# A hand-written engine order for the first 32 units of an attention and FFN kernel, with the weights' low words converted in place

## The chip, the cores and the metric

The kernel runs on one core of one Trainium2 chip. The metric is the device time of one execution in microseconds (us). A core has a matrix engine (TensorE, PE in the profile), whose weight loads are listed apart as PEld, and three engines for element-wise work: VectorE (DVE), ScalarE (ACT) and GpSimd (POOL). SyncE (SP) issues the transfers between HBM and the core's memory. Each engine works through its own queue in order; an instruction waits for others by semaphores.

## The reference, cut to what matters

Local and global attention over 8 batches, 8 heads, 512 local and 32 global tokens, head size 64; its output, 4352 rows of 512, goes through a feed-forward network with a leaky activation, all in fp32.

```python
s_g = scale * q_g @ k_all.T            # global tokens see all 544 keys
out_g = softmax(s_g) @ v_all
s_ll = where(abs(i - j) <= 32, scale * q_l @ k_l.T, -1e9)
s_lg = scale * q_l @ k_g.T
out_l = softmax(concat([s_lg, s_ll])) @ concat([v_g, v_l])
x = concat([out_g, out_l])             # rows of 8 heads * 64
h = x @ w_in                           # 512 -> 2048
g = maximum(h, 0) + alpha * minimum(h, 0)
out = g @ w_out                        # 2048 -> 512
```

The weights are handed to the kernel as 64-bit floating-point numbers. Each is decoded on the chip from its high and its low 32-bit word into an fp32 number, which is then split into a rounded part and the rest, so that three TensorE products stand for one exact fp32 product.

## The kernel before, in words

The program is one loop over units u = 0 to 164, written out in full. An attention job is a pair of heads P (32 pairs: four for each batch), and every pair takes four units, s = 0 to 3 (P, s = divmod(u, 4)). From unit 19 on (NPRE) a unit also carries one step t = u - 19 of the feed-forward network: `f1(t)` multiplies 128 hidden channels for a batch of 512 rows (12 matmuls into the PSUM tile h_ps, two buffers), and `f2(t-2, part)` takes the activated result of two steps before into the four output banks (12 matmuls, tiles o). Sixteen steps make a batch, and batch b needs pairs 4b to 4b+3. The first 19 units hold attention alone, and in them `keep_warm` issues five matmuls on a zeroed tile per unit.

Pairs below 8 (NRAW) take the "raw" path, which this change is mostly about. At s=0 six score blocks of two heads are multiplied, masked and exponentiated (`scores_raw`, `softmax`: one DVE instruction and one ACT exponential each, lines 202 to 207); at s=1 the last two blocks follow, along with the transposed global probabilities of the pair before (`transpose_glb`, `copy_glb`, line 286); at s=2 the pair before is multiplied with its values (`pv_raw`), the global scores are multiplied (`global_scores`) and `pv_out` copies the result out (lines 359 to 367); then `global_softmax` runs a chain of five small DVE instructions, an exponential, four small DVE instructions and a scaling (lines 267 to 277). The `tail` of a softmax (lines 209 to 216) adds an epsilon on ACT, takes the reciprocal on DVE and normalizes the eight blocks on ACT; for pair 0 three of them run on GpSimd (line 214). At s=3 TensorE transposes the probabilities (`transpose_pe`), ACT copies them (line 302) and DVE transposes the small remainders (line 315). Pairs share one p_sb and one pt_sb buffer. Pairs from 8 on take another path, by way of HBM.

Weights come in 32 pieces of 128x512 numbers, two for each of the 16 hidden blocks. A piece is loaded six pieces ahead (`load_weights`, line 99), decoded by `decode_words` (two ACT instructions, lines 107 and 108, three on DVE, lines 109 to 112, a GpSimd addition, line 114), and one unit later split by `split_weights` (ACT, line 120, GpSimd, line 121). From unit 3 on the pace is one piece in two units out of three; from unit 19 on one or two in turn (RATE).

The order on TensorE is the written one: `matmul` and `transpose` pin every instruction behind the one before. On ACT, DVE, GpSimd and in the queue of DMA issues, a planner orders the instructions by its own estimate of their times, with higher priority for attention from unit 4 on (`boost`). Scratch tiles of 128x512 come from one ring of 18 buffers, tag "st" (`stage`): the two decode tiles wt and wr, the activation tiles g, gh and gl, the split inputs xh and xl, the tile vx of extra values of a raw pair, a mask and an identity. Larger tiles come from 33 buffers of the pool wpool: raw and split weights, and rawk.

Of the kernel before, what the change touches and what calls it, by code (L numbers as in the profile page):

```python
# [38 lines left out]
NPRE = 19  # L39
LAG = 2  # L40
WFIRST = 3
RATE = ((1, 1, 0), (2, 1))
# [9 lines left out]

@with_exitstack
def longformer_ffn(ctx: ExitStack, tc: tile.TileContext, qk, qkr, gn, vt, vx, w, alpha, out):
    nc = tc.nc
    PS = bass.MemoryType.PSUM
# [46 lines left out]
    def decode_words(f, j):  # L103
        words = wraw.pop((f, j)).rearrange("p (n two) -> p n two", two=2)
        low, high = words[:, :, 0], words[:, :, 1]
        t, r = stage("wt"), stage("wr", I32)
        nc.scalar.activation(t, high.bitcast(F32), AF.Abs)  # L107
        nc.scalar.activation(r, low, AF.Copy, scale=2.0**-29)
        nc.vector.tensor_scalar(t, t, CLAMP_LO, CLAMP_HI, op0=ALU.max, op1=ALU.min)  # L109
        tu = t.bitcast(U32)  # L110
        nc.vector.tensor_scalar(tu, tu, 3, 0x3FFFFFFF, op0=ALU.logical_shift_left, op1=ALU.bitwise_and)  # L111
        nc.vector.scalar_tensor_tensor(tu, high, 0xC0000000, tu, op0=ALU.bitwise_and, op1=ALU.bitwise_or)  # L112
        ti = t.bitcast(I32)
        nc.gpsimd.tensor_tensor(ti, ti, r, op=ALU.add)  # L114
        wmid[f, j] = t

    def split_weights(f, j):
        t = wmid.pop((f, j))
        wt = wpool.tile([128, 2, 512], F32R, tag="w", name="wt")
        nc.scalar.copy(wt[:, 0, :], t)  # L120
        nc.gpsimd.tensor_tensor(wt[:, 1, :], t, wt[:, 0, :].bitcast(F32), op=ALU.subtract)
# [9 lines left out]
    nc.vector.memset(rmask[0:64, 0, 0:32], NEG)  # L131
    nc.vector.memset(rmask[64:128, 2, 128:160], NEG)
# [5 lines left out]
    nc.vector.memset(idle.bitcast(F32), 0.0)  # L138
# [25 lines left out]
    def load_v(P):  # L164
# [4 lines left out]
        if P < NRAW:  # L169
            vxs[P] = stage("vx").rearrange("p (i n) -> p i n", i=4)  # L170
            nc.sync.dma_start(vxs[P], vx[P])
# [5 lines left out]
    def prep_qk(P, h, part):  # L177
# [6 lines left out]
        nc.scalar.copy(t, raw)  # L184
        if part == 0:
            q = t[64:128]
            nc.gpsimd.tensor_tensor(q, raw[64:128], q.bitcast(F32), op=ALU.subtract)  # L187
        else:
            kl[P, h] = work.tile([128, NK], F32R, tag="kl", name="kl", bufs=2)
            nc.gpsimd.tensor_tensor(kl[P, h], raw, t.bitcast(F32), op=ALU.subtract)  # L190
# [8 lines left out]
    def softmax(parts, npool=0):  # L199
        n = len(parts)  # L200
        mn, z, rz = small("mn", 6), small("z", 6), small("rz", 6)
        for e, (src, mk, pr) in enumerate(parts):
            nc.vector.tensor_tensor_reduce(  # L203
# [3 lines left out]
            nc.scalar.activation(pr, pr, AF.Exp, bias=mn[:, e : e + 1], scale=-1.0, accum_out=z[:, e : e + 1])  # L207

        def tail():
            nc.scalar.activation(rz[:, 0:n], z[:, 0:n], AF.Copy, bias=1e-9)  # L210
# [276 lines left out]
    def attn_mid(u):  # L487
# [4 lines left out]
        if P >= NRAW:  # L492
            while tails:
                tails.pop()()
# [158 lines left out]
```

## Time and profile before

| | us |
|---|---|
| median of 3 runs | 1026.85 (1025.22 to 1028.45) |
| the profiled execution | 1027.97 |
| its span, first to last instruction | 1026.20 |

The mean granted TensorE clock of the profiled execution is 0.972 of full speed. Busy over the span: PE 980.9 us, DVE 624.0, ACT 528.3, GpSimd 410.9. In the profile's rows a group reads as line, engine, operation, tiles written and read, shape and count, then busy time, mean ns of one, and the idle time ahead of them with what ended it. Rows of the view by windows give busy time of each engine in a stretch, with the granted clock (PEclk) and the share of the DMA engines in use.

### The profile page before, as it was taken

What the parts mean: (1) busy time and instruction counts of PE and PEld (TensorE: products, weight loads), DVE (VectorE), ACT (ScalarE), POOL (GpSimd) and SP (SyncE); (2) the same over time, 40 slices, a digit from 0 to 9 for tenths busy, and PEclk for the clock granted to TensorE, in tenths of its full rate; (3) what the DMA queues carried; (4) which work ended last, traced back from release to release, by engine and by line L of the source; (5) the groups of instructions that cost most, each with busy time, mean ns of one, the idle gap of its engine ahead of it and who ended that gap; (6) DMA issues with size and microseconds to landing.
All of it is one profiled execution on the core that took longest, in us unless ns stands there. A gap on an engine that the chain in (4) does not pass through costs nothing.

```text
span 1026.2 us, 16973 instructions
## 1 busy us (share of the span) xinstructions
PE 980.9 (96%) x5615; PEld 792.2 (77%) x5615; DVE 624.0 (61%) x1975; ACT 528.3 (51%) x1476; POOL 410.9 (40%) x332
## 2 busy tenths in 40 slices
PE   5589998879999999999999999999999999999998
PEld 3356776658888888888888888888888888888798
DVE  7735878776666766676666666666667665322322
ACT  5676767556555655555556555555556543201121
POOL 6601676764344443334434344334434422222222
PEclk8688999889999999999999999999999999999999
DMA  9624522234544544555445544554445532100010
GB/s 348 248 82 142 189 100 92 80 91 143 151 151 144 168 151 142 151 152 174 142 143 160 181 141 141 152 173 144 134 145 179 152 108 84 42 1 1 1 43 21
DMA packets 95274, 133.00 MB, mean 130 GB/s; under 512 B 10193, under 2 KB 53713, under 8 KB 95185
## 3 DMA queue, kind: packets, MB, share of 16 engines
q1 hardware_dynamic: 95184, 131.91, 41.1%
q8 instruction: 44, 0.72, 0.3%
q14 instruction: 46, 0.37, 0.1%
HBM read 100.93 MB, written 30.93 MB: 129 GB/s over the span
## 4 chain that ended last, share of the span: by engine, by line
PE 83%; DVE 7%; ACT 5%; issue 2%; DMA 1%; POOL 1%; SPq 0%; DVEq 0%; ACTq 0%; POOLq 0%
PE h_ps L84 35%; PE o L84 34%; PE o_ps L84 5%; PE s_ps L84 4%; PE g_ps L84 3%; ACT p_sb L207 2%; DVE wt L112 1%; DVE wt L109 1%; DVE wt L111 1%; PE warm L84 1%; ACT p_sb L216 1%; DMA wraw<-in_w_dram 1%; ACT wt L107 1%; DVE g L395 1%; DVE pt_sb L315 1%
## 5 line engine op out<-in xcount | busy, mean ns | idle before, releaser
L84 PE MATMUL h_ps<-xh,wt 128*128 128x512 f32 (+1 forms) x1152 | 350.4, 387 | 5.5 <-ACT wt L120 3.1
L399 POOL TENSOR_TENSOR gl<-g,gh 128x512 fp32r<-128x512 f32 (+1 forms) x144 | 177.6, 1233 | 426.6 <-ACT gh L398 378.1
L84 PE MATMUL o<-gh,wt 128*128 128x512 f32 (+1 forms) x1152 | 284.9, 390 | 0.0
L84 PEld LDWEIGHTS o<-gh,wt 128*128 128x128 f32 x1152 | 208.0, 190 | 45.6 <-issue 0.7
L84 PEld LDWEIGHTS h_ps<-xh,wt 128*128 128x128 f32 x1152 | 206.9, 190 | 44.5 <-ACT wt L120 3.3
L398 ACT CAST gh<-g 128x512 fp32r<-128x512 f32 (+1 forms) x144 | 85.3, 593 | 273.3 <-DVE g L396 266.2
L84 PE MATMUL h_ps<-xl,wt 128*128 128x512 f32 (+1 forms) x576 | 221.9, 385 | 0.9 <-DVE xl L378 0.9
L395 DVE TENSOR_SCALAR g<-h_ps,alpha_sb 128x512 f32<-128x512 f32 (+1 forms) x144 | 103.2, 717 | 147.1 <-PE h_ps L84 143.5
L84 PE MATMUL o<-gl,wt 128*128 128x512 f32 (+1 forms) x576 | 151.2, 385 | 0.0
L207 ACT ACTIVATE p_sb<-p_sb,mn 128x224 f32<-128x224 f32 (+2 forms) x256 | 115.0, 451 | 45.2 <-DVE mn L203 45.2
L216 ACT ACTIVATE p_sb<-p_sb,rz 128x192 f32<-128x192 f32 (+1 forms) x253 | 100.3, 451 | 71.7 <-DVE rz L211 66.8
L84 PEld LDWEIGHTS h_ps<-xl,wt 128*128 128x128 f32 x576 | 109.1, 189 | 24.4 <-DVE xl L378 1.1
L84 PEld LDWEIGHTS o<-gl,wt 128*128 128x128 f32 x576 | 106.4, 191 | 23.7
L297 DVE STREAM_TRANSPOSE pt_sb<-sg_sb 32x64 f32<-32x64 f32 x384 | 90.5, 236 | 26.8 <-ACT sg_sb L277 21.5
L187 POOL TENSOR_TENSOR hi<-rawq,hi 64x512 fp32r<-64x512 f32 x48 | 62.4, 1300 | 86.9 <-DMA vt<-in_vt_dram 53.6
L396 DVE SCALAR_TENSOR_TENSOR g<-h_ps,g 128x512 f32<-128x512 f32 (+1 forms) x144 | 94.0, 653 | 3.0
L203 DVE CUSTOM_DVE_ANT_0 p_sb<-s_ps,mask 128x192 f32<-128x192 f32 x192 | 65.2, 369 | 28.3 <-PE s_ps L84 27.5
L190 POOL TENSOR_TENSOR kl<-rawk,hi 128x640 fp32r<-128x640 f32 x48 | 75.7, 1577 | 3.6
L84 PE MATMUL o_ps<-pt_sb,vt 128*64 128x160 f32 (+3 forms) x768 | 62.1, 294 | 15.6 <-ACT pt_sb L286 15.6
L84 PEld LDWEIGHTS o_ps<-pt_sb,vt 128*64 128x64 f32 (+2 forms) x768 | 45.8, 138 | 32.5 <-ACT pt_sb L286 17.2
L211 DVE RECIPROCAL rz<-rz 128x2 f32<-128x2 f32 (+1 forms) x112 | 18.5, 165 | 74.6 <-ACT rz L210 73.7
L114 POOL TENSOR_TENSOR wt<-wt,wr 128x512 int32<-128x512 int32 x32 | 41.9, 1310 | 53.3 <-DVE wt L112 36.0
(86 smaller groups left out, 1039.9 us busy)
## 6 DMA issues: line engine op xcount, KB each, us to landing
scratch<-p_sb SPq DMA_DIRECT2D x192, 112.0 KB, 2.3
wraw<-in_w_dram SPq DMA_DIRECT2D x32, 512.0 KB, 7.8
vt<-in_vt_dram SPq DMA_DIRECT2D x32, 512.0 KB, 5.0
rawk<-in_qk_dram SPq DMA_DIRECT2D x96, 160.0 KB, 3.0
rawq<-in_qk_dram SPq DMA_DIRECT2D x96, 128.0 KB, 2.7
pt_sb<-scratch SPq DMA_DIRECT2D x48, 256.0 KB, 2.7
gn<-in_gn_dram SPq DMA_DIRECT2D x32, 304.0 KB, 5.2
pt_sb<-scratch SPq DMA_DIRECT2D x48, 192.0 KB, 2.9
```

Of the source, the lines that this page charges most:

```text
L84: tc.keep_in_program_order(nc.tensor.matmul(*a, **k))
L114: nc.gpsimd.tensor_tensor(ti, ti, r, op=ALU.add)
L187: nc.gpsimd.tensor_tensor(q, raw[64:128], q.bitcast(F32), op=ALU.subtract)
L190: nc.gpsimd.tensor_tensor(kl[P, h], raw, t.bitcast(F32), op=ALU.subtract)
L203: nc.vector.tensor_tensor_reduce(out=pr, in0=src, in1=mk, scale=-0.125, scalar=3.0e38, op0=ALU.add, op1=ALU.min, accum_out=mn[:, e : e + 1],)
L207: nc.scalar.activation(pr, pr, AF.Exp, bias=mn[:, e : e + 1], scale=-1.0, accum_out=z[:, e : e + 1])
L216: nc.scalar.activation(r, r, AF.Copy, scale=rz[:, e : e + 1])
L297: nc.vector.transpose(dst, src)
L395: nc.vector.tensor_scalar(g[:, 0:n], h[:, 0:n], 0.0, alpha_sb[:, f : f + 1], op0=ALU.min, op1=ALU.mult)
L396: nc.vector.scalar_tensor_tensor(g[:, 0:n], h[:, 0:n], 0.0, g[:, 0:n], op0=ALU.max, op1=ALU.add)
L398: nc.scalar.copy(gh[:, 0:n], g[:, 0:n])
L399: nc.gpsimd.tensor_tensor(gl[:, 0:n], g[:, 0:n], gh[:, 0:n].bitcast(F32), op=ALU.subtract)
```

## The change: what it does

A wrapper `Ordered` pins ACT, DVE and GpSimd instructions behind the one before on the same engine, as long as a flag is set; the flag is set for units below 32 (WRITTEN). For these units the loop body is a new sequence. Instructions of later units, and the issuing of DMAs, stay with the planner.

```python
class Ordered:
    def __getattr__(self, name):
        op = getattr(self._engine, name)
        def call(*a, **k):
            ins = op(*a, **k)
            if self._on[0]:
                self._tc.keep_in_program_order(ins)
            return ins
        return call
...
        written[0] = u < WRITTEN
        if u < WRITTEN:
            raw_head(u)
            weights_first(u)
            if t >= 0:
                f1(t)
            weights_split()
            if t >= 1:
                leaky(t - 1)
            raw_norms(u)
            attn_pre(u)
            if u in XSPLIT:
                split_x(0, XSPLIT.index(u))
            attn_mid(u)
            if last:
                split_x(G, NC - 1)
            if t >= LAG:
                f2(t - LAG, 0)
                f2(t - LAG, 1)
            weights_rest()
            attn_post(u)
            if u < NWARM:
                keep_warm(WARM)
            continue
```

The parts of it:

- The decode is cut in two. `weights_first` holds the DMA issue and the two ACT instructions, at the head of the unit; `weights_rest` holds the three DVE instructions and the GpSimd addition, behind the unit's attention. `weights_split` (of the unit before) lies between.
- The activation is cut out of `f1` as `leaky(t)`; below unit 32 it is written one unit later, behind the matmuls of `f1(t)` and ahead of that unit's attention.
- The tail of a raw softmax is cut up. `raw_head` takes the reciprocals of the unit before (s=1, s=2) and the sum of the global softmax (s=3); `raw_norms` normalizes three blocks at s=1, five at s=2, and scales the global probabilities at s=3. `global_softmax` becomes `global_exp`, `global_sum` and `global_scale`. The three blocks of pair 0 on GpSimd go to ACT.
- The input splits of the first batch (`split_x`) stand in units 8, 12 and 16 (XSPLIT), and after unit 18's attention.
- The low word is turned into an integer in place, `r = low.bitcast(I32)`, so the ring tile wr goes, and the GpSimd addition reads every second word of the raw tile, which is kept until then.
- The tile vx of pairs 0 to 5 comes from wpool and no longer from the ring.

```diff
-        t, r = stage("wt"), stage("wr", I32)
-        nc.scalar.activation(t, high.bitcast(F32), AF.Abs)
-        nc.scalar.activation(r, low, AF.Copy, scale=2.0**-29)
+        t, r = stage("wt"), low.bitcast(I32)
+        act.activation(t, high.bitcast(F32), AF.Abs)
+        act.activation(r, low, AF.Copy, scale=2.0**-29)
...
+    def raw_head(u):
+        P, s = divmod(u, 4)
+        if s == 1:
+            rest[P, 0][0]()
+        if s == 2:
+            rest[P, 1][0]()
+            held[P] = pair_banks(u, ("o_ps", "g_ps"))
+            global_bank(P, held[P][1])
+        if s == 3:
+            global_sum(P)
+
+    def raw_norms(u):
+        P, s = divmod(u, 4)
+        if s == 1:
+            rest[P, 0][1](0, 3)
+        if s == 2:
+            rest.pop((P, 0))[1](3, 6)
+            rest.pop((P, 1))[1](0, 2)
+        if s == 3:
+            global_scale(P)
```

209 lines of the change are left out of this document (128 added, 81 removed).

## The prediction

> **What bounds the kernel now.** I read the view by windows first, cut at the score matmuls of pairs 0 to 4 (5.40, 23.30, 51.60, 68.50, 82.20), at the first f1 (95.90), at the 17th (231.00), after one more group of four units, and after the last pair.
>
> ```profile
> core 0: us, PE busy (x) PEld busy (x) DVE busy (x) ACT busy (x) POOL busy (x), PEclk, DMA share, GB/s
> ...
> 5.40:23.30 17.90, 12.94 (x67) 7.76 (x67) 13.38 (x42) 15.16 (x41) 10.78 (x13) 0.78 1.03 394
> 23.30:51.60 28.30, 17.54 (x117) 11.50 (x116) 22.68 (x58) 18.01 (x50) 19.31 (x16) 0.66 0.67 258
> 51.60:68.50 16.90, 15.42 (x117) 10.07 (x116) 6.82 (x39) 11.09 (x40) 1.92 (x2) 0.80 0.26 87
> 68.50:82.20 13.70, 12.61 (x117) 8.30 (x116) 6.63 (x38) 9.96 (x36) 1.27 (x1) 1.00 0.36 122
> 82.20:95.90 13.70, 12.58 (x105) 7.93 (x105) 6.64 (x36) 9.56 (x34) 0.00 (x0) 0.80 0.33 105
> 95.90:231.00 135.10, 120.09 (x729) 91.61 (x729) 105.43 (x249) 86.83 (x225) 88.01 (x68) 0.93 0.35 114
> 231.00:258.10 27.10, 27.10 (x152) 22.28 (x152) 17.75 (x66) 16.41 (x47) 10.85 (x8) 1.00 0.47 139
> 258.10:860.30 602.20, 602.20 (x3328) 495.32 (x3327) 390.63 (x1362) 333.82 (x948) 236.43 (x174) 1.00 0.50 150
> 860.30:1026.20 165.90, 160.41 (x897) 137.38 (x895) 51.24 (x88) 27.41 (x56) 37.59 (x36) 1.00 0.07 22
> ```
>
> From 231.00 to 860.30 PE is busy without a gap (27.10 of 27.10, 602.20 of 602.20), so nothing on ACT, DVE or GpSimd can shorten it, and 860.30 to 1026.20 has neither pairs nor decoding. All that the change can win or lose lies in the first 231.00: 95.90 ahead of the first f1 (**the lead-in**), and 135.10 for the steps t=0 to 15 (**the decode stage**). In the lead-in the pairs take 17.90, 28.30, 16.90 and 13.70, though their attention is the same but for the edges; where GpSimd is busy, with 19.31 in the pair of 28.30, weights are being decoded.
>
> Next, the timeline of PE in the decode stage (start, duration, and in brackets the wait ahead with its end): first f1 of t=9 to 12, with f2 of t=9's unit between, then three waits.
>
> ```profile
> 162.76 0.64 PE L84 MATMUL h_ps<-xh,wt 128*128 128x512 f32 x2
> ...
> 166.64 2.14 PE L84 MATMUL o<-gh,wt 128*128 128x512 f32 x8
> ...
> 169.55 0.64 PE L84 MATMUL h_ps<-xh,wt 128*128 128x512 f32 x2
> ...
> 175.97 0.64 PE L84 MATMUL h_ps<-xh,wt 128*128 128x512 f32 x2
> ...
> 185.68 0.64 PE L84 MATMUL h_ps<-xh,wt 128*128 128x512 f32 x2
> ...
> 194.15 1.12 PE L87 MATMUL pt<-ident,p_sb 128*128 128x128 f32 x4 [5.05 <-ACT sg_sb L272]
> ...
> 216.02 0.50 PE L84 MATMUL h_ps<-xh,wt 128*128 128x512 f32 x1 [3.10 <-ACT wt L120]
> 218.88 0.80 PE L84 MATMUL h_ps<-xh,wt 128*128 128x512 f32 x1 [2.37 <-POOL wt L121]
> ```
>
> Undisturbed units start 6.79, 6.42 and 9.71 apart (s=0, s=1, s=2). For s=3 I take s=1's 6.42, as its eight small transposes are of the size of s=1's ten small matmuls. Sixteen units then need 4 x (6.79 + 6.42 + 9.71 + 6.42) = 117.4. Steps 0 and 1 have no f2, which runs from 166.64 to 169.55, so 2 x 2.9 goes off: 111.6. The stage took 135.10; 23.5 is lost, and the last rows show to what: the global softmax (5.05) and the split of weights that f1 needs at once (3.10, 2.37).
>
> **The change, part by part.** The prices of the work that is reordered, from the groups of the first 210 us:
>
> ```profile
> L114 POOL TENSOR_TENSOR wt<-wt,wr 128x512 int32<-128x512 int32 x30 | 39.2, 1307 | 52.6 <-DVE wt L112 35.3 <-ACT p_sb L207 8.8 <-ACT wt L107 2.3
> L121 POOL TENSOR_TENSOR wt<-wt 128x512 fp32r<-128x512 f32 x29 | 38.7, 1342 | 11.7 <-ACT wt L120 8.1 <-issue 1.7 <-POOL gl L399 1.6
> ...
> L399 POOL TENSOR_TENSOR gl<-g,gh 128x512 fp32r<-128x512 f32 x14 | 18.6, 1331 | 4.7 <-PE s_ps L84 1.8 <-DVE mn L203 1.7 <-ACT gh L398 1.2
> ...
> L107 ACT ACTIVATE wt<-wraw 128x512 f32<-128x512 f32 x32 | 21.1, 660 | 3.4 <-POOL wt L114 2.6 <-POOL gl L399 0.8
> L108 ACT ACTIVATE wr<-wraw 128x512 int32<-128x512 uint32 x31 | 20.7, 666 | 0.3 <-PE o L84 0.3
> ...
> L120 ACT CAST wt<-wt 128x512 fp32r<-128x512 f32 x29 | 17.6, 612 | 5.7 <-POOL wt L114 5.7
> ...
> L109 DVE TENSOR_SCALAR wt<-wt 128x512 f32<-128x512 f32 x31 | 22.2, 716 | 15.9 <-ACT wt L107 15.7
> ...
> L111 DVE TENSOR_SCALAR wt<-wt 128x512 uint32<-128x512 uint32 x31 | 28.1, 910 | 0.5
> L112 DVE SCALAR_TENSOR_TENSOR wt<-wraw,wt 128x512 uint32<-128x512 uint32 x31 | 27.5, 887 | 0.6
> ...
> L395 DVE TENSOR_SCALAR g<-h_ps,alpha_sb 128x512 f32<-128x512 f32 x14 | 10.4, 743 | 4.8 <-PE h_ps L84 2.0 <-POOL gl L399 1.6 <-POOL wt L121 1.2
> ...
> L396 DVE SCALAR_TENSOR_TENSOR g<-h_ps,g 128x512 f32<-128x512 f32 x14 | 9.5, 682 | 0.2
> ```
>
> A piece costs ACT 0.66 + 0.67 + 0.61 = 1.94, DVE 0.72 + 0.91 + 0.89 = 2.51, GpSimd 1.31 + 1.34 = 2.65. The DVE figure holds waits for GpSimd, as the timeline shows:
>
> ```profile
> 10.53 0.43 DVE L109 TENSOR_SCALAR wt<-wt 128x512 f32<-128x512 f32 x1 [1.67 <-ACT wt L107]
> ...
> 10.99 0.43 DVE L111 TENSOR_SCALAR wt<-wt 128x512 uint32<-128x512 uint32 x1
> ...
> 11.45 0.69 DVE L112 SCALAR_TENSOR_TENSOR wt<-wraw,wt 128x512 uint32<-128x512 uint32 x1
> ```
>
> ```profile
> 39.02 1.26 POOL L114 TENSOR_TENSOR wt<-wt,wr 128x512 int32<-128x512 int32 x1 [0.69 <-DVE wt L112]
> ...
> 39.04 1.53 DVE L111 TENSOR_SCALAR wt<-wt 128x512 uint32<-128x512 uint32 x1
> ```
>
> Alone the three take 0.43 + 0.43 + 0.69 = 1.55. The L111 that starts beside GpSimd's L114 ends only 0.29 after it, so most of its 1.53 was waiting.
>
> *Lead-in, first pair.* The normalization of three blocks on GpSimd goes to ACT. The waits of the first 100 us (total, times, longest), and the timeline of a later pair's eight:
>
> ```profile
> PE pt L87 <- POOL p_sb L214: 4.0, 2, 3.6
> ```
>
> ```profile
> 57.97 2.65 ACT L216 ACTIVATE p_sb<-p_sb,rz 128x160 f32<-128x160 f32 x8
> ```
>
> PE waited 4.0 for it; on ACT three blocks are 3 x 2.65 / 8 = 1.0. No piece is decoded ahead of unit 3, where GpSimd was busy for 10.78 of the first pair's 17.90. So pair 1's scores come at 23.3 - 3.0 = 20.3.
>
> *Lead-in, later pairs.* Pair 3 (68.50 to 82.20) has no decoding and takes 13.70 at a granted clock of 1.00; pair 2, with hardly more on DVE and GpSimd (6.82, 1.92), takes 16.90 at 0.80. That is the attention alone, warm and cold. Eleven pieces now fall in units 3 to 18, 2.75 to a pair. I take as hidden the ACT part at s=0 and s=2 (beside the score matmuls and `pv_raw`), and GpSimd's part throughout, which only the next unit's split waits for. On the chain lie the ACT part at s=1, between the exponentials and `copy_glb`, for which `pv_raw` waits, in two units of three: 0.67 x 1.94 = 1.3; and the DVE part at s=2 and s=3, queued ahead of the global sum and of the next pair's maskings, as the queue is fixed: 2 x 0.67 x 2.51 = 3.4. That makes 18.4 a pair warm and 21.6 cold; I take 19, near the warm one, as ACT's exponential runs beside the first of the two DVE parts and `keep_warm` stays. The ends are 13.7 (warm, all hidden) and 13.7 + 2.75 x (1.94 + 2.51) = 25.9 (nothing hidden). Three pairs put pair 4's scores at 20.3 + 57 = 77.3; from there to f1 were 13.7, now with 1.3 more: f1 starts at 92.3, **3.6 earlier**.
>
> What goes is pair 1's stall, here in the chain of waits (start, duration):
>
> ```profile
> 28.80 7.14 DMA wraw<-in_w_dram
> ```
>
> Before, an ACT instruction of the decode was queued ahead of pair 1's exponentials and stood still until its piece had landed (28.80 + 7.14). Late next is DVE's decode.
>
> *Decode stage.* Does each engine's work fit under PE's 29.3 for four units? DVE: attention 6.63 (the pair of 68.50), four activations of 0.74 + 0.68 = 5.7, six pieces at 2.51 = 15.1, in all 27.4. ACT: 9.96, four casts like L120 (2.4), six pieces 11.6, in all 24.0. GpSimd: four times 1.33 and six pieces, 21.2. All fit. Now the waits that a fixed queue adds. `leaky(t-1)` stands on DVE behind the decode of the unit before and a reciprocal that waits for ACT; behind it are the maskings. PE asks for its result (gh, gl) in the next unit's f2, and for the h_ps buffer at the next unit's f1, so one unit of 6.4 or more covers a DVE unit of 27.4 / 4 = 6.9 on average; if that cover goes, PE waits for the difference. Work on ACT and DVE for the banks of a unit has f2 and the next f1 (5.8) to hide behind. The weights come in time: 30 of 32 pieces are begun by unit 31, and f1(15), which waited 3.10 + 2.37, has two units from its piece's begin. I keep one such wait, 5.5, for the change-over at unit 32, where the planner takes over with two pieces left. So 111.6 + 5.5 = 117.1, **18.0 less**.
>
> *In-place integers and buffers.* One wait for a ring tile goes, by the waits of the decode stage:
>
> ```profile
> ACT wt L107 <- POOL wt L114: 2.6, 2, 1.3
> ```
>
> That is 2.6 at most, off PE's path, so I book nothing. ACT's write at every second word and GpSimd's read of it have no row; the nearest is ACT's read of every second word, 0.66 (L107) against 0.61 packed (L120), so from nothing to, at the far end, a doubling of the addition, 1.3 for each of six: GpSimd 29.0 in four units, just under PE's 29.3. I take nothing, as L107 is nearest. The raw tile is held longer by the addition's 1.31, with 33 buffers and at most 32 pieces loaded or split: nothing. The ring of 18 is full with mask and identity (2), xh and xl (8), three decode tiles and five of g, gh, gl; a ninth in the last group waits for the f2 of three steps back, done when the unit begins: nothing, else up to 2.9 a unit.
>
> *Moved transfers.* The weights' issues are written ahead of the pair's loads, but SP keeps the planner's order; the loads run six pieces ahead, four units at the least, against 7.14 to land. The input splits move forward to where GpSimd idles (1.27 busy in the pair of 68.50): nothing.
>
> *Sum.* 92.3 + 117.1 + 27.1 + 602.2 + 165.9 = 1004.6 of span, 21.6 less than 1026.2. The profiled execution took 1027.97, 1.77 more than its span; the median is 1026.85, 1.12 under that execution. Forecast: 1026.85 - 21.6 = **1005.2**.
>
> **Rivals.** *The shared port.* If DVE's decode and GpSimd never overlap, units 19 to 31 hold 19 pieces at 2.65 + 1.55 and 12 steps of 1.33, 95.8, against PE's 111.6 - 22.9 (units 32 to 34) = 88.7. That adds 7.1: 1012. For it speak L111's 1.53; against it, that the written order puts DVE's activation and softmax, which read PSUM, beside GpSimd's splits. The Trainium skill (GPSIMD Engine Reference, "Key points") says so as a rule: GpSimd shares its memory interface with DVE instructions in a two-port mode or with two inputs from SBUF; the 1.53 agrees.
>
> *Nothing hidden in the lead-in.* At 25.9 a pair f1 starts at 20.3 + 77.7 + 15.0 = 113.0, 20.7 later than forecast: 1026, no change. Against it: 13.70 for the bare attention leaves ACT idle 3.7 of it and DVE 7.1.
>
> *Cold pairs.* If all pairs take the 21.6 of the low clock, f1 starts at 20.3 + 64.8 + 15.0 = 100.1, 7.8 later than forecast: 1013. For it: three of the five pairs ran at 0.80 or less; against it: the one at 1.00 had no more warming matmuls than they. The Trainium skill (TensorE: Matmul & The Clock Gate, "Part 1: The HAM clock gate") halves the array's clock after an idle window of about 3.4 us, which speaks against an order that lets PE wait for ACT and DVE; 0.80 beside 16.90 and 1.00 beside 13.70 agree in kind.
>
> *Hand-offs in the decode stage* (the slower side). A fixed queue cannot step past a waiting instruction. If each unit's decode on DVE (19 pieces in 13 units, 1.46 x 2.51 = 3.67) stands unhidden ahead of the activation or masking that PE needs next, PE waits 13 x 3.67 = 47.7 where I left 5.5: 1047. It decides from (21.6 + 5.5) / 13 = 2.1 a unit on. For it: DVE's 27.4 of 29.3 leaves little play. Against it: two h_ps buffers and two steps between f1 and f2.
>
> *Given back at the change-over.* At unit 31 the second head of pair 8 is prepared in the fixed order, and it has one rawq buffer (the page's DMA issues, KB each and us to landing):
>
> ```profile
> rawq<-in_qk_dram SPq DMA_DIRECT2D x96, 128.0 KB, 2.7
> ```
>
> ACT's copy there waits for a transfer of 2.7 that starts when GpSimd is through with the first head, and behind it on ACT stands the copy of pair 7's transposes. With 2.37 more for the last split that is 5.1: 1010.
>
> **How the numbers follow.** The forecast has 0.46, the port 0.16, cold pairs 0.08, the change-over 0.06, the unhidden lead-in 0.11, the hand-offs 0.13. A difference under 0.3% (3 us) can't be told from none. The first four are faster, with 0.02 of the unhidden lead-in: 0.78. Of that lead-in 0.06 is no change, and 0.03 with the hand-offs slower: 0.16. The low end has pairs of 15 (12 less) and the stage at its floor (5.5 less): 1005.2 - 17.5 = 988. The high end takes in the port, the change-over, cold pairs and the lead-in case: 1027. Left out are the hand-offs and little else.
>
> **What would show it.** Right: pair 1's scores near 20, the next ones some 19 apart, f1 from about 92, the 17th f1 about 22 earlier, PE's waits there for splits and the global softmax gone, the rest alike, L114 still at 1.31. Wrong: pairs over 24 apart in the lead-in, with PE waiting for `copy_glb` or the transposes; PE waits of 2 us or more in each unit from 19 to 31 for gh, gl or h_ps; L109 to L112 longer than 2.51 together; L114 near 2; a gap of PE past 231.

## The result, and the profile after

The changed kernel takes 1041.9 us (median of 4 runs, 1041.51 to 1041.97) beside 1026.03 for the kernel before on the same chip: a ratio of 1.0156, 95% interval 1.0127 to 1.0185. It is slower, and the forecast of 1005.2 was wrong in sign. The profiled span grew from 1026.2 to 1039.8, by 13.6; the medians differ by 15.9, mostly because the profiled execution of the kernel before (1027.97) lies 1.9 above its median. The kernel before spreads more than the changed one, 1022.36 to 1031.39 in 29 runs, so a difference of 2 or 3 us against one profile of it says little.

The view by windows of the changed kernel, cut at the same events as before: score matmuls of pairs 0 to 4, first f1 (107.90), 13th f1 (199.90), 14th (213.80), 17th (244.40), one more group, last pair.

```profile
core 0: us, PE busy (x) PEld busy (x) DVE busy (x) ACT busy (x) POOL busy (x), PEclk, DMA share, GB/s
5.60:20.50 14.90, 12.68 (x66) 7.96 (x66) 6.19 (x37) 11.09 (x35) 1.26 (x4) 0.89 1.03 383
20.50:41.40 20.90, 16.02 (x117) 10.37 (x116) 10.73 (x39) 12.23 (x40) 6.00 (x5) 0.76 0.52 184
41.40:65.40 24.00, 16.05 (x121) 10.38 (x120) 12.36 (x48) 13.70 (x43) 9.05 (x8) 0.72 0.39 134
65.40:88.30 22.90, 16.76 (x117) 11.05 (x116) 14.54 (x54) 16.70 (x49) 7.98 (x7) 0.70 0.42 150
88.30:107.90 19.60, 13.92 (x104) 8.88 (x104) 8.02 (x34) 11.42 (x40) 6.76 (x5) 0.72 0.39 133
107.90:199.90 92.00, 85.27 (x553) 63.48 (x553) 78.79 (x184) 65.10 (x171) 59.34 (x45) 0.99 0.35 120
199.90:213.80 13.90, 7.64 (x38) 6.16 (x36) 13.23 (x26) 7.30 (x14) 10.00 (x9) 0.85 0.30 100
213.80:244.40 30.60, 26.42 (x141) 20.23 (x141) 18.50 (x43) 15.49 (x40) 18.76 (x15) 0.85 0.33 96
244.40:271.50 27.10, 27.10 (x152) 22.26 (x151) 17.39 (x65) 16.40 (x47) 10.83 (x8) 1.00 0.46 141
271.50:873.70 602.20, 602.20 (x3327) 494.72 (x3327) 390.82 (x1362) 333.79 (x948) 236.32 (x174) 1.00 0.50 150
```

From the 17th f1 on nothing has changed (27.10 and 602.20 again). The lead-in is 12.0 longer (107.9 for 95.9), the decode stage 1.4 (136.5 for 135.1). The first pair is the shortest of the lead-in, 14.90; the pairs behind it take 20.90, 24.00 and 22.90, and no engine is busy for all of that: in the last of them PE has 16.76 of 22.90 and ACT 16.70. So the engines wait in turn. The view of PE's waits in the first 108 us (total, times, longest; first the row of the kernel before, up to its first f1, then that of the changed kernel) and the changed kernel's ACT group of the weights' casts in the first 246 (busy, mean ns, idle time ahead and what ended it):

```profile
PE o_ps L84 <- ACT pt_sb L286: 14.5, 4, 10.8
```

```profile
PE o_ps L104 <- ACT pt_sb L63: 24.6, 4, 7.9
```

```profile
L63 ACT CAST wt<-wt 128x512 fp32r<-128x512 f32 x32 | 19.7, 618 | 39.9 <-POOL wt L63 37.5 <-POOL kl L63 2.3
```

PE waits once per pair for ACT's copy of the transposed global probabilities (`copy_glb`), 24.6 in all. In the kernel before it was 14.5, of which 10.8 belong to the one pair that stalled. And ACT stands still for 37.5 ahead of casts whose input GpSimd has not finished, 14.5 of it in the lead-in; in the kernel before it was 5.7 for 29 of the 32 casts. The timeline of one pair in the changed kernel shows how the one makes the other (start, duration, wait ahead):

```profile
45.10 0.69 DVE L63 SCALAR_TENSOR_TENSOR wt<-wraw,wt 128x512 uint32<-128x512 uint32 x1
45.71 0.32 DVE L63 CUSTOM_DVE_ANT_0 p_sb<-s_ps,rmask 128x160 f32<-128x160 f32 x1
...
45.87 1.29 POOL L63 TENSOR_TENSOR wt<-wt,wraw 128x512 int32<-128x512 int32 x1 [2.01 <-DVE wt L63]
...
47.20 0.62 ACT L63 CAST wt<-wt 128x512 fp32r<-128x512 f32 x1 [3.32 <-POOL wt L63]
47.72 0.61 ACT L63 CAST xh<-x_raw 128x512 fp32r<-128x512 f32 x1
...
48.24 0.42 ACT L63 ACTIVATE p_sb<-p_sb,mn 128x160 f32<-128x160 f32 x1
...
54.13 0.74 PE L104 MATMUL o_ps<-pt_sb,vt 128*64 128x96 f32 x4 [7.95 <-ACT pt_sb L63]
```

The unit's first masked scores were ready at 45.71 + 0.32, but the exponential begins at 48.24. Ahead of it in ACT's queue stands the cast of the piece decoded in the unit before, and that piece is late: DVE ended it at 45.79, GpSimd's addition at 47.16. ACT did not step past. (The cast xh behind it, 0.61, is the input split of this unit; the masking itself stands behind DVE's part of the decode, which the prediction had priced.) The exponentials, the normalization, `copy_glb` and PE's product follow, each late. That this wait is the cause, and how much of it, the experiments have to say.

### The profile page after: what moved, and what is told of

It is laid out like the page before. It is cut to its first block, busy times and chain, and to the rows that moved or that the text cites. A ratio compares the mean times of both kernels' runs of the same rounds, so it can differ in the third digit from the quotient of the medians.

```text
span 1039.8 us, 16938 instructions
## 1 busy us (share of the span) xinstructions
PE 985.0 (95%) x5615; PEld 793.2 (76%) x5615; DVE 624.4 (60%) x1975; ACT 530.6 (51%) x1479; POOL 408.8 (39%) x329
## 4 chain that ended last, share of the span: by engine, by line
PE 82%; DVE 10%; ACT 4%; POOL 2%; issue 2%; DMA 1%; SPq 0%; DVEq 0%; ACTq 0%; POOLq 0%
PE o L104 34%; PE h_ps L104 34%; PE o_ps L104 6%; DVE wt L63 5%; PE s_ps L104 4%; PE g_ps L104 4%; ACT p_sb L63 2%; POOL wt L63 1%; DVE g L63 1%; DVE pt_sb L63 1%; DVE p_sb L63 1%; DVE gz L63 1%; DVE gm L63 1%; ACT wt L63 1%; DMA qk_raw<-in_qkr_dram 0%
## 5 line engine op out<-in xcount | busy, mean ns | idle before, releaser
L104 PE MATMUL o<-gh,wt 128*128 128x512 f32 (+1 forms) x1152 | 282.0, 387 | 0.0
L63 ACT ACTIVATE p_sb<-p_sb,rz 128x224 f32<-128x224 f32 (+2 forms) x256 | 101.7, 450 | 73.7 <-DVE rz L63 67.9
L63 DVE STREAM_TRANSPOSE pt_sb<-sg_sb 32x64 f32<-32x64 f32 (+1 forms) x448 | 103.3, 231 | 27.9 <-ACT sg_sb L63 21.5
L104 PE MATMUL o_ps<-pt_sb,vt 128*64 128x160 f32 (+3 forms) x768 | 65.5, 305 | 25.1 <-ACT pt_sb L63 25.0
L63 POOL TENSOR_TENSOR wt<-wt,wraw 128x512 int32<-128x512 int32 x32 | 42.2, 1319 | 94.0 <-DVE wt L63 33.7
## 6 DMA issues: line engine op xcount, KB each, us to landing
rawq<-in_qk_dram SPq DMA_DIRECT2D x96, 128.0 KB, 2.7
```

The lines of the kernel that those rows point to most:

```text
L63: ins = op(*a, **k)
L104: tc.keep_in_program_order(nc.tensor.matmul(*a, **k))
```

## The experiments

First f1 is the start of the first feed-forward matmul, the stage runs from there to the 17th. One profiled execution each; where more runs were made, the ratio to the kernel before with its 95% interval. Experiments without a ratio rest on one run.

| run | span | first f1 | stage | ratio |
|---|---|---|---|---|
| before | 1026.2 | 95.9 | 135.1 | |
| changed kernel | 1039.8 | 107.9 | 136.5 | 1.0156 (1.0127 to 1.0185) |
| e1_split_late | 1032.5 | 100.9 | 136.3 | |
| e2_bare_lead | 1014.1 | 85.5 | 133.7 | |
| e3_pin_lead | 1042.5 | 108.5 | 138.6 | |
| e4_pin_stage | 1026.6 | 94.5 | 136.8 | |
| e5_buffers_only | 1022.8 | 93.5 | 134.5 | |
| e6_leaky_first | 1047.4 | 107.5 | 144.4 | |
| e7_prep_late | 1038.8 | 107.4 | 136.5 | |
| e8_hidden_decode | 1024.2 | 100.5 | 128.1 | |
| e9_piece_early | 1033.0 | 108.5 | 129.7 | 1.0094 (1.0061 to 1.0127) |
| e10_stage_and_piece | 1021.8 | 99.5 | 127.5 | 0.9969 (0.9951 to 0.9987) |
| e11_before_and_piece | 1020.9 | 94.9 | 130.8 | 0.9965 (0.9942 to 0.9988) |
| e12_warm_eight | 1038.1 | 106.8 | 135.9 | |
| e13_split_late_32 | 1021.8 | 98.0 | 127.8 | 0.9972 (0.9953 to 0.9991) |
| e14_split_and_prep_late | 1020.9 | 99.5 | 126.1 | 0.9953 (0.9936 to 0.9969) |
| e15_all_late | 1023.3 | 99.9 | 128.0 | 1.0006 (0.9988 to 1.0025) |

### The lead-in

**e1_split_late.** In the units of the lead-in the split is written behind attention.

```diff
-            weights_split()
+            if u >= NPRE:
+                weights_split()
...
             attn_mid(u)
+            if u < NPRE:
+                weights_split()
```

> In the first 19 units the split of the piece before (cast on ACT, subtraction on GpSimd) is written behind the unit's attention and no longer ahead of it; all else as after the change. Theory A (the cast stands in ACT's fixed queue ahead of the exponentials and the global scaling and waits for DVE's decode and GpSimd's addition of the unit before): pairs of 20.9 to 24.0 us fall to 18 to 20, the first f1 comes at 95 to 100 instead of 107.9, the span at 1028 to 1032. Rival B (the three DVE instructions ahead of the global sum and the maskings are the cost, as the prediction booked them): those stay where they are, so less than 1 us a pair, f1 not before 105. Rival C (the low granted clock, 0.6 to 0.7 for most of the lead-in): no change beyond 2 us either.

The first f1 comes at 100.9, 7.0 earlier, and PE's wait for the copy shrinks, as its waits up to 101 us show:

```profile
PE o_ps L104 <- ACT pt_sb L63: 16.5, 4, 6.4
```

The stage stays as it was. So the place of the split, the cast on ACT with GpSimd's subtraction behind it, costs 7.0 of the 12.0 us that the lead-in lost. The other 5.0 no experiment takes apart.

**e2_bare_lead.** No piece is decoded in the lead-in; GpSimd sets the split tiles of these pieces to zero.

```diff
+        if (f, j) in plain:
...
+            pool.memset(wt.bitcast(F32), 0.0)
...
...
-            decode_first(*pieces[i])
+            if u < NPRE:
+                plain.add(pieces[i])
+            else:
+                decode_first(*pieces[i])
```

> The pieces that would be decoded in the first 19 units are left out: their transfers stay, but no ACT, DVE or GpSimd instruction decodes them, and GpSimd sets their split tiles to zero. Theory A and rival B: without decode the pairs of the lead-in take 14 to 16 us, the first f1 comes near 80. Rival C (clock) and rival D (the written order of the attention itself is slow, without any weights): pairs stay over 18, f1 after 92. The steps from f1 on should stay near 136 for the first 16 by all of them.

The windows of e2_bare_lead, pairs 1 to 3 and from pair 4's scores to the first f1:

```profile
21.50:36.00 14.50, 12.62 (x121) 8.30 (x120) 5.55 (x35) 8.66 (x34) 0.00 (x0) 1.00 0.83 295
36.00:53.40 17.40, 15.35 (x119) 10.04 (x119) 7.73 (x42) 11.15 (x39) 3.07 (x3) 0.80 0.54 182
53.40:70.60 17.20, 15.32 (x117) 9.94 (x116) 6.52 (x39) 9.88 (x37) 3.95 (x4) 0.80 0.46 161
70.60:85.50 14.90, 13.03 (x104) 8.19 (x104) 4.49 (x29) 8.39 (x34) 3.07 (x3) 0.77 0.59 209
```

Attention alone in the written order takes 14.50 at a granted clock of 1.00 and 17.4 and 17.2 at 0.80, on average 16.4 a pair. PE's own busy time makes the difference, 12.62 against 15.35 and 15.32 for about as many matmuls; its idle time is 1.9 to 2.1 in all three. But the two longer pairs also carry an input split each, as the units 8 and 12 do and no unit of the first has, so the clock is not the only thing that differs. Decoding eleven pieces adds 107.9 - 85.5 = 22.4, 2.0 a piece; with e1's order it adds 15.4, 1.4 a piece.

**e3_pin_lead and e4_pin_stage.** The order is pinned in the units below 19 alone, or in units 19 to 31 alone.

```diff
-        written[0] = u < WRITTEN
+        written[0] = u < NPRE              # e3
+        written[0] = NPRE <= u < WRITTEN   # e4
```

> The sequence is as after the change, but the instructions of units 19 to 31 are no longer pinned: the planner orders them. If the pinned queue costs the decode stage (the prediction's hand-off rival), the first 16 steps fall from 136.5 us to 120 or less. If what holds them is common to both orders (DVE and GpSimd sharing their time, the full buffers at unit 30 to 34, the pace of the pieces), they stay between 130 and 140. f1 stays at 106 to 109, as the lead-in is pinned as before.

> The sequence is as after the change, but only units 19 to 31 are pinned; the lead-in is ordered by the planner. If the loss of 14 us lies in the pinned lead-in alone, f1 comes at 94 to 98 and the span at 1026 to 1030. If the new sequence itself (cut tails, split decode) makes the lead-in longer however it is ordered, f1 stays over 103. The first 16 steps stay at 134 to 139.

With the lead-in alone pinned the first f1 is at 108.5, with it left to the planner at 94.5. So the lead-in's loss is the pinning, not the new text of the loop, which both have. The stage takes 138.6 with the planner's order and 136.8 pinned: its first twelve steps fall from 99.7 to 90.3, and its last four, where the written order hands over to the planner, rise from 39.0 to 46.5.

**e5_buffers_only.** The kernel before with the change's integers in place and vx from the other pool, and no order.

```diff
-        t, r = stage("wt"), stage("wr", I32)
+        t, r = stage("wt"), low.bitcast(I32)
...
-            vxs[P] = stage("vx")...
+            vxs[P] = (stage("vx") if P >= NRAW - 2 else wpool.tile(...))...
```

> The kernel before, in the planner's order throughout, with only the buffers of the change: low words turned to integers in place, and the extra values of pairs 0 to 5 in the larger pool. If GpSimd pays for reading every second word (the prediction's far end), its addition goes from 1.31 to over 1.8 us. If not, it stays within 0.05 of 1.31, ACT's write stays near 0.67, and the span moves by what the planner makes of it, within 5 us of 1026. If these buffers were the cause of the loss, the span is over 1036.

It took 1024.64 beside 1023.67 for the kernel before. The buffers and the integers by themselves are not the cause.

**e12_warm_eight.** WARM = 8 in place of 5.

> The changed kernel with eight idle multiplications per lead-in unit instead of five. Theory 'the clock' : in the changed kernel's lead-in the TensorE's granted clock is 0.73-0.76 from 20 to 100 us (0.76-0.83 in the kernel before from 40 on), and the pairs' 20-24 us come from transposes and products at the lower clock; with three more idle multiplications a unit the granted clock rises over 0.85 and the pairs fall to 17-19 us, first f1 90-96, time 1024-1030. Rival 'the queue of ScalarE' (the casts of the unit before stand ahead of the exponentials): the clock may rise but the pairs stay within 1.5 us of theirs; the added multiplications stand in the TensorE's queue behind the unit's own and cost up to 0.7 us a unit: first f1 105-118, time 1039-1052.

The windows of e12_warm_eight, pairs 1 to 3 and the stretch to the first f1:

```profile
20.80:43.50 22.70, 19.89 (x129) 13.28 (x128) 12.77 (x47) 13.60 (x43) 7.78 (x6) 0.77 0.60 206
43.50:65.50 22.00, 18.56 (x129) 12.12 (x128) 11.26 (x45) 13.13 (x42) 8.44 (x7) 0.84 0.37 126
65.50:88.20 22.70, 19.93 (x129) 13.13 (x128) 14.14 (x50) 16.16 (x48) 7.24 (x7) 0.77 0.36 127
88.20:106.80 18.60, 15.42 (x114) 9.88 (x113) 7.11 (x32) 11.47 (x39) 6.30 (x5) 0.82 0.43 153
```

The clock rises from 0.70-0.76 to 0.77-0.84 and PE is busier by some 3 us a pair, but pairs 1 to 3 take 67.4 instead of 67.8. The added matmuls fill PE's waits (its wait for the copy in the lead-in falls from 24.6 to 12.2), and nothing behind them ends sooner. So a clock higher by this much gives no time here. What a clock of 1.00 would give, no run with decoding shows: the rival of the clock is weakened and not settled.

**e8_hidden_decode.** The whole decode is moved to where DVE was thought idle: one piece at s=0, two at s=1, none behind, splits at the end of s=3; 12 pieces instead of 11 before the first f1.

```diff
+        n = (1, 2, 0, 0)[u % 4] if u < NPRE else RATE[1][u % len(RATE[1])]
...
             attn_mid(u)
+            if u < NPRE and u % 4 == 3:
+                weights_split()
+            if u < NPRE and u % 4 == 1:
+                weights_first(u)
...
-            weights_rest()
+            if u >= NPRE or u % 4 < 2:
+                weights_rest()
```

> As after the change, but in the lead-in the decode is placed where ACT and DVE wait in each pair: one piece at s=0 (ACT's part at the head of the unit, DVE's behind the maskings), two at s=1 behind the copies for which the values wait, none at s=2 and s=3, and the splits at the end of s=3; 12 pieces instead of 11. Bare attention in this order took 14.5 to 17.4 us a pair, f1 at 85.5. Theory A with the DVE term (the whole excess over the bare order is decode standing on the pair's chain): pairs of 16 to 18.5, f1 at 86 to 92, span 1018 to 1024. Rival G (DVE and GpSimd hinder each other wherever the decode stands): pairs over 20, f1 after 98.

It was a miss in the lead-in: 100.5 where I expected 86 to 92, and where the rival that DVE and GpSimd hinder each other said over 98. Its timeline shows one reason:

```profile
60.69 3.96 POOL L63 TENSOR_TENSOR wt<-wt 128x512 fp32r<-128x512 f32 x3 [6.71 <-ACT wt L63]
...
62.40 2.53 DVE L63 TENSOR_SCALAR wt<-wt 128x512 f32<-128x512 f32 x2
...
64.61 1.44 POOL L63 TENSOR_TENSOR xl<-x_raw,xh 128x512 fp32r<-128x512 f32 x1
...
64.96 1.64 DVE L63 SCALAR_TENSOR_TENSOR wt<-wraw,wt 128x512 uint32<-128x512 uint32 x1
66.52 0.18 DVE L63 RECIPROCAL rz<-rz 128x6 f32<-128x6 f32 x1
```

Three GpSimd subtractions of weights and one of the input now run beside DVE's decode, which takes 4.17 instead of the 0.89 + 0.69 that it takes elsewhere in the lead-in, and the softmax's reciprocal waits behind it in DVE's queue. Another reason is in PE's waits: for DVE's clearing of the g_ps bank, which stands behind the two pieces of s=1, PE waits 8.4 in the lead-in, where it is 2.6 in e2. How the miss divides between them was not measured. The stage, however, fell to 128.1, which I had not looked for; the next runs follow that.

### The decode stage

**e6_leaky_first.** `leaky(t - 1)` is written first in its unit.

```diff
+            if t >= 1:
+                leaky(t - 1)
             raw_head(u)
             weights_first(u)
...
             weights_split()
-            if t >= 1:
-                leaky(t - 1)
```

> As after the change, but the activation of the step before stands at the head of each unit from 20 to 31, ahead of the reciprocals, the global sum, the decode's ACT part and the split. Theory E (in the units of s=3 and s=1 the activation waits behind the global sum or a reciprocal, and PE for the h_ps buffer behind it: 6.2 us in 5 waits): those waits go, units of 8.3 at s=3 become 6.4 to 6.9, and the first 16 steps 130 to 132 instead of 136.5. Rival (DVE's total is the limit in these units, by its decode beside GpSimd): the waits turn up elsewhere, and the steps stay within 2 us of 136.5.

The stage grew to 144.4. PE's waits for the activation did fall, from 6.2 to 2.6, but two of the three units of s=2 went from about 10 to 16.3 and 16.9. Behind the activation, at the head of its queue, ACT's cast gh waits for DVE, 30.9 in all where it was 6.6, with the normalization and the copies behind it; PE waits for the copies in both units, 1.98 and 2.81. That is the smaller part: in the first of the two PE is busy for 14.32, at a granted clock of 0.69, where the changed kernel has 9.85 at 1.00 in the same unit. That theory fell, and the wait cost less than the low clock behind it.

**e7_prep_late.** In the last written unit the casts of the next pair's query and key stand behind attention.

```diff
-            if live(P + 1) and P + 1 >= NRAW:
+            if live(P + 1) and P + 1 > NRAW:
...
             attn_mid(u)
+            if u == WRITTEN - 1:
+                prep_qk(NRAW, 1, 0)
+                prep_qk(NRAW, 1, 1)
```

> As after the change, but in unit 31 the second head of pair 8 is prepared behind the unit's copies of the transposes and no longer ahead of them. Theory F (ACT's queue holds the copy that frees the banks behind these casts and a split that waits for GpSimd): PE's wait of 6.3 us at the first score of pair 8 falls to 3 to 4.5, the 13th step from 13.9 to 11 to 12, and the end follows by 2 us at least. Rival (the last split weights set the pace there, 2.9 + 1.3 at the 16th step): what is won at unit 31 is lost at unit 34, and the first 16 steps stay within 1 us of 136.5.

The 13th step fell from 13.88 to 12.52, and the next ones gave it back: 136.5 as before.

**e9_piece_early.** Decoding begins at unit 1 instead of 3, which puts 12 pieces ahead of the first f1 instead of 11.

```diff
-WFIRST = 3
+WFIRST = 1
```

> The changed kernel with one more weight piece decoded ahead: decoding begins in the second unit instead of the fourth, so 12 pieces are ready by the 19th unit instead of 11; nothing else differs. Theory 'the fixed pace': in the changed kernel units 14 and 15 of the decode stage (9.36 and 14.04 us between starts of the first multiplications) wait for the last pieces, and not for attention; with one piece more in hand both come near the least that the TensorE needs (about 6.3 and 10.1), the stage from the first f1 to the 17th goes from 136.5 to 128-130 us. The lead-in pays for the piece only if a chain waits for it; the first pair waits for its transfer at that time anyway: first f1 107-110. Time 1033-1036 us. Rival 'attention at the change-over': the two units wait for the score or transposition chain of the last written unit, and one more piece moves only the name of what is late: stage 135-137, time 1040-1044.

The windows of e9_piece_early, cut at the first, 13th, 14th and 17th f1:

```profile
108.50:200.40 91.90, 85.79 (x554) 63.86 (x554) 78.47 (x184) 64.81 (x171) 59.41 (x45) 0.98 0.33 115
200.40:214.20 13.80, 7.56 (x37) 6.09 (x36) 13.13 (x26) 7.31 (x14) 9.94 (x9) 0.87 0.29 101
214.20:238.20 24.00, 24.00 (x143) 18.86 (x142) 16.88 (x40) 14.40 (x38) 16.31 (x13) 0.93 0.42 122
```

The last three steps take 24.00, with PE busy for all of it, where they took 30.60. In the changed kernel the waits in them are 4.2, and PE was busy for 26.42 at a granted clock of 0.85, against 24.00 at 0.93 here. What PE waited for in the changed kernel is in its waits from 200 to 246 us:

```profile
PE s_ps L104 <- ACT pt_sb L63: 6.3, 1, 6.3
PE h_ps L104 <- ACT wt L63: 2.9, 1, 2.9
PE h_ps L104 <- POOL wt L63: 1.3, 1, 1.3
```

The last two, for the last split, are gone with one piece in hand; the first belongs to the 13th step. The pace of the decode was one piece too short, and the piece itself cost the lead-in 0.6.

**e10_stage_and_piece and e11_before_and_piece.** The same edit on e4, and on the kernel before.

> Two things together: the written order holds only from the 20th unit (the lead-in is left to the planner, as in e4_pin_stage, 1028.75 us), and decoding begins in the second unit as in e9_piece_early. If the lead-in's loss comes from the pinned order there and the stage's loss from the last pieces, the two add: first f1 about 95-97, stage 128-130, time 1019-1023 us, under the kernel before (1026) by over half a percent. Rival: the planner, given one more piece in the lead-in, puts it into the chain of a pair as it stands (about 2 us a piece) and the stage shows the loss at the change-over to planned units in another place (stage 135-137): time 1027-1031.

> The kernel before, with decoding begun in the second unit instead of the fourth. Its own units 14 and 15 after the first f1 take 9.55 and 15.02 us. Theory 'the fixed pace': these are the same wait for the last pieces as in the changed kernel, whatever keeps the order; stage 127-130 instead of 135.1, first f1 95-98, time 1018-1022 us. Rival: the kernel before loses there by the planner's own order, and the piece decoded early is paid in the first pair's chain, which is late already: stage 133-136, time 1025-1029.

On e4 the stage gains 9.3, but the planner's lead-in pays 5.0 for the piece. On the kernel before the stage gains 4.3: its 15th step falls from 9.55 to 6.28, the 16th stays long (14.55). So the piece is missing in both orders, though in the planner's it is not all that the last steps lack.

**e13_split_late_32 and e14_split_and_prep_late.** What stays is the 13th step, 13.9, in which PE waits 6.3 for ACT's copies of the transposed probabilities. In the changed kernel two casts of weights stand ahead of them in ACT's queue, and wait for GpSimd:

```profile
206.32 0.62 ACT L63 CAST wt<-wt 128x512 fp32r<-128x512 f32 x1 [2.71 <-POOL wt L63]
...
209.28 0.62 ACT L63 CAST wt<-wt 128x512 fp32r<-128x512 f32 x1 [2.33 <-POOL kl L63]
```

e13 moves the last written unit's split behind attention on e10, e14 moves e7's two casts as well.

```diff
-            weights_split()
+            if u != WRITTEN - 1:
+                weights_split()
...
             attn_mid(u)
+            if u == WRITTEN - 1:
+                prep_qk(NRAW, 1, 0)        # e14 only
+                prep_qk(NRAW, 1, 1)        # e14 only
+                weights_split()
```

> e10_stage_and_piece (1022.5 us) with one move: in the 32nd unit, the last written one, the casts of the unit before's two weight pieces stand behind attention in ScalarE's queue instead of ahead of it. Theory 'casts ahead of the copies': in that unit ScalarE waits 2.7 us for GpSimd's addition and 2.3 us for a ring buffer that GpSimd frees, and the copies of the transposed probabilities, for which the TensorE waits 6.3 us, start only behind them; with the casts behind, the step of 13.9 us falls to 8-9.5, the stage from 127.5 to 122.5-124, time 1017-1020. Rival 'the other casts': the four casts of query and key of the next pair that stand ahead too wait for GpSimd in their turn, and the step stays over 11.5; what is gained comes back in the next units, whose weights are later: stage 126-128, time 1021-1024.

> As e13_split_late_32, and the casts and subtractions of the first planned pair's second query and key also stand behind attention in the 32nd unit (the edit of e7_prep_late, which gained 1.4 us at the 13th step and lost it behind, when the last pieces were late anyway). Theory 'casts ahead of the copies': 13.9 falls to 7-8.5, and with a piece in hand it is not given back: stage 121-123, time 1016-1019. Rival: the scores of that pair now wait for the late query and key, and the unit behind takes what this one gave: stage 125-128, time 1020-1024.

e13 missed: the step stays at 13.93. ACT's timeline in e13_split_late_32 names what stands ahead of the copies when the split is gone:

```profile
190.99 0.68 ACT L63 ACTIVATE wraw<-wraw 128x512 int32<-128x512 uint32 x1
196.34 0.62 ACT L63 CAST gh<-g 128x512 fp32r<-128x512 f32 x1 [4.67 <-DVE g L63]
196.87 0.53 ACT L63 ACTIVATE sg_sb<-sg_sb,gz 128x288 f32<-128x288 f32 x1
199.06 0.62 ACT L63 CAST hi<-rawq 128x512 fp32r<-128x512 f32 x1 [1.66 <-DMA rawq<-in_qk_dram]
199.58 0.72 ACT L63 CAST hi<-rawk 128x640 fp32r<-128x640 f32 x1
200.21 1.06 ACT L63 COPY pt_sb<-pt 128x512 f32<-128x512 f32 x2
```

Three waits lay one behind the other, and taking away the first, for GpSimd, let the others show: 4.67 for DVE's activation, then 1.66 for the transfer into the single rawq buffer. e14 takes the transfer's wait from ahead of the copies as well; its step takes 11.01 and the one behind it 8.49, the stage 126.1. The activation's wait is left, and with it 3.4 of PE's.

**e15_all_late.** The changed kernel with the whole order written and e1's, e9's and e14's edits together.

> The changed kernel with the whole order written up to the 32nd unit, and the three edits together: 12 pieces in the lead-in, the lead-in's weight casts behind attention (as in e1_split_late, 1034.6), the 32nd unit's casts behind it too (as in e14_split_and_prep_late). If the parts add: first f1 101, stage 122-124, time 1020-1024, about level with the kernel before (1023.5). Rival: in the lead-in the late casts and the twelfth piece collide, first f1 104-107, time 1026-1031.

The first f1 is at 99.9, the stage takes 128.0, and the time is that of the kernel before (1.0006). The three repairs together account for 16.5 of span; they take back the loss and no more. The fastest version by its median is e14, at 1020.94 beside 1025.16 for the kernel before, a ratio of 0.9953. It and e11, which has no written order, can't be told apart by their intervals.

## Why the prediction was wrong, step by step

**First pair: right.** Pair 1's scores came at 20.5 (forecast 20.3), and PE's wait for GpSimd's normalization is gone. GpSimd is busy for 1.26 of the pair, where it was 10.78.

**Later pairs: the step that failed first.** I booked GpSimd's part as hidden, "which only the next unit's split waits for". That sentence holds the mistake: the split is a cast at the head of ACT's queue, so a cast that waits for GpSimd there holds the exponentials. I had named what is queued behind the wait for DVE and not for ACT. Pairs 1 to 3 took 67.8 instead of 57, and the stretch from pair 4's scores to f1 19.6 instead of 15.0. Of these 15.4, the decode has 6.2: against e2 it added 18.7 to the three pairs and 4.7 behind them, 23.4, where I had 3 x 5.3 + 1.3 = 17.2. In e1, with the casts behind, it added 16.6, near the 17.2 in sum; whether ACT's and DVE's parts were each right, no run shows. The other 9.2, the larger term, is the bare attention, 49.1 for three pairs and 14.9 behind them in e2, where I took 13.7 for each. I had read that from the one pair of the kernel before that ran at a granted clock of 1.00; in e2 a pair at 1.00 took 14.50, and only one in three ran there. So I also failed in taking a value near the warm one.

**Decode stage: the cover failed, and the copies at the change-over were put at nothing.** Forecast 117.1, measured 136.5, 19.4 more. The first twelve steps took 92.0 against 82.2 of floor. Of these 9.8, 5.9 are four waits for an h_ps buffer that DVE's activation had not yet freed, which is the cover that I said would have to hold (6.9 of DVE against a unit of 6.4). Two of the four, in the changed kernel's timeline:

```profile
126.01 0.73 PE L104 MATMUL h_ps<-xh,wt 128*128 128x512 f32 x2 [1.72 <-DVE g L63]
...
144.33 0.73 PE L104 MATMUL h_ps<-xh,wt 128*128 128x512 f32 x2 [1.69 <-DVE g L63]
```

Of the other 3.9, 1.25 lie in the first step, 4.77 against 6.42 - 2.9 = 3.52, which starts at a granted clock of 0.50 (up to 110.4); the rest no run takes apart. The last four steps took 44.5 against 34.9 with the wait that I had allowed. The wait for splits, for which the 5.5 stood, was 2.9 + 1.3. What I had at nothing is the 6.3 in front of the scores, for ACT's copies, and a PE that is busy for 34.1 (7.64 + 26.42) where the floor has 29.3, at a granted clock of 0.85. Only in a rival had I let these copies be late, by 2.7. e9 takes 6.8 off the stage, the missing piece: I counted pieces begun by unit 31, and not when the last of them would be split. e14's stage is 1.4 shorter than e10's, by one profile each, for the casts ahead of the copies.

**Integers in place, buffers, transfers: right, but for one wait.** GpSimd's addition, now reading every second word, took 1.319 (mean of 32) against 1.310, and e5 shows no cost beyond the spread of single runs. The pool of 33 buffers, for which I booked nothing, shows one wait: the cast that waits 2.3 for GpSimd's subtraction kl, the last reader of a buffer of that pool. Moving the cast (e13) gave no time, so on the path it cost nothing by itself.

**The rest: right.** From the 17th f1 to the end of the span it was 795.4 against 795.1.

**The rivals.** For the first f1 "Nothing hidden in the lead-in" was nearest, 113.0 against the 107.9 measured, but not by its terms: it had 13.7 of attention and 12.2 of decode in a pair, and measured were 16.4 (e2) and 18.7 / 3 = 6.2. "Cold pairs", with 16.9 and 4.7, was nearer in both, and its 21.6 nearer to the 22.6 of a pair; e12 does not confirm the clock as the cause, and does not exclude it. "Given back at the change-over" was right in place. With the 5.5 of the forecast its 5.1 makes 10.6, and the waits were 10.5 (6.3 + 2.9 + 1.3); but it had 2.7 for the copies and 7.9 for the splits, so the agreement of the sums is luck. "Hand-offs in the stage" comes nearest in time (1047) and not by its mechanism: it needed 3.67 in each of 13 units, and PE's waits for DVE's activation are 6.2 in all. I had let each case fail alone, with the others at their forecast; the lead-in and the change-over failed together. The rule of the Trainium skill cited for "Cold pairs" (TensorE: Matmul & The Clock Gate, "Part 1: The HAM clock gate") agrees in kind with e2's 14.50 at 1.00 and 17.2 at 0.80. "The shared port" is seen, below, but what it costs the stage was not measured by itself. The forecast's own signs of failure, pairs near 24 apart with PE waiting for `copy_glb`, are what the profile showed.

## What to carry to other kernels

When an order is written by hand, follow each handed-over value through every queue that it enters: an instruction that is cheap and "hidden" on its own engine holds all that stands behind its consumer, and a step that reaches over to another engine and back belongs behind the urgent work of its unit. Before crediting an order with time, count stock against need at the deadline: one more piece decoded ahead brought the kernel before to 0.9965, and the best written order, with that piece, 0.9953, which the intervals do not tell apart. After moving one waiting instruction, expect the next in the queue to wait almost as long.

## What the runs showed of the hardware that was not expected

A tiny DVE instruction can last as long as a GpSimd instruction beside it. In the changed kernel's lead-in:

```profile
40.53 1.30 POOL L63 TENSOR_TENSOR wt<-wt,wraw 128x512 int32<-128x512 int32 x1 [11.01 <-ACT wt L63]
40.61 1.23 DVE L63 SCALAR_TENSOR_TENSOR gz<-gz 64x1 f32<-64x1 f32 x1
41.87 0.62 ACT L63 CAST wt<-wt 128x512 fp32r<-128x512 f32 x1 [1.32 <-POOL wt L63]
41.88 0.15 DVE L63 RECIPROCAL gz<-gz 64x1 f32<-64x1 f32 x1
```

The sum of one number per partition took 1.23, and ended with GpSimd's addition, within 0.02. Up to 210 us the changed kernel has this instruction eight times: twice with no GpSimd instruction beside it, at 0.15, and six times beside an addition begun just before it, at 1.17 to 1.25, each ending 0.01 to 0.02 after the addition. In e1_split_late one that began later beside it took 0.93. So in these cases its length is what is left of GpSimd's instruction, whatever its own size. The maskings at 45.71 and behind, which read the scores from PSUM, took 0.32 each beside an addition, as without one at 51.40. The Trainium skill (GPSIMD Engine Reference, "Key points") has the rule that the prediction set beside the 1.53 of the decode; it names DVE instructions with two inputs from SBUF, which this sum is, and the trace agrees.

Also, after PE's wait of 6.3 at the change-over the matmuls of f1 ran slowly for a few us. Two of them, from the changed kernel's timeline:

```profile
213.80 1.08 PE L104 MATMUL h_ps<-xh,wt 128*128 128x512 f32 x2
...
221.00 0.64 PE L104 MATMUL h_ps<-xh,wt 128*128 128x512 f32 x2
```

Two matmuls of this kind took 1.08 right behind the wait and 0.64 one step later. The granted clock was 0.50 from 209.6 to 216.2 and 1.00 from 216.4 to 229.9, so by this reading the wait on PE cost more than its own length. e6 shows it more strongly: its first long unit has a wait of 1.98, and PE's busy time in it is 4.47 longer at a granted clock of 0.69. In both the low clock comes with the wait; no run holds the two apart.
